# Three edits joined in a fused attention and routed feed-forward kernel: the last blocks' value products in a row, the last routing one half behind the other, four fill products at the branch's end

## The chip, the cores and the metric

The kernel runs on one core of a Trainium2 chip. The metric is the time of the device in microseconds (us), the median of several runs; lower is better. Five engines work in order, each on its own queue, and meet at semaphores: PE (TensorE, matrix products into PSUM), DVE (VectorE), ACT (ScalarE), POOL (GpSimd) and SP (SyncE, which issues most transfers). PE's clock has two levels, 2.4 GHz (a granted clock of 1.00 in the profile) and 1.2 GHz (0.50).

## What is computed

```python
# attention, for 4 batches x 8 heads, 768 tokens, head width 64
scores = q @ k.T / sqrt(64)
keep = (key position < n_sink) | (0 <= query - key < window)      # 4 and 128
a = softmax(where(keep, scores, -1e9)); x = a @ v                 # heads joined: 4 x 768 x 512
# routing, token by token
logits = x @ w_gate                                               # 8 experts
fresh = argmax(logits); local = sigmoid(x @ w_local)
e = fresh if first token or local < 0.5 else the expert of the token before
# one expert for each token
out = p[e] * (relu(x @ w1[e]) @ w2[e])                            # 512 -> 1024 -> 512, p = softmax(logits)
```

All in fp32. A product that needs fp32's precision is built from three products of halves: each operand is split into a high part (a cast, "fp32r") and a low part (the rest, a subtraction), and high x high, high x low and low x high are added up in PSUM.

## The kernel before

**Attention.** The 3072 tokens are 24 blocks of 128 per half of the heads, in 8 groups (4 batches x 2 halves of 4 heads), 48 blocks in all. Each block needs scores (L643), bias and mask on DVE (L655), exponentials on ACT (L658), transposes of them on PE (L673, copied by ACT at L680, `turned`), value products (L709, `apply`), a copy of those by DVE (L595, `collect`), a product that turns them back and gives the routing's logits (L599, `back`), and a division by the sums on DVE (L615, `ending`). The loop `for n in range(nb)` writes PE, DVE and ACT out by hand: in iteration n the scores of block n, the transposes of block n-1, the value products of block n-2 and the return of block n-3. POOL splits the next group's heads in the first two blocks of a group (L135, L140).

**Routing.** `routing()` returns small steps, most of them some DVE instructions on up to 48 elements: logits, `best`, `fresh`, `powers` (exponentials), a turn by PE and a `scan` for the expert carried on from token to token, `totals`, a turn back, `join` and `chosen` (the one-hot of the expert, L337 and L338), `gates` (L349 to L351), `ranks` (PE) and `slots`/`send`, and six scatters on POOL (L376), which write 128 rows each to a buffer in DRAM sorted by expert. The tables `ROUTE` and `ROUTE_L` say in which block behind a batch's last one each step is issued; the steps write into a free strip of a score bank. The last batch is routed in two halves, `head_r` and `tail_r`, in the straight code behind the loop.

**End of the attention branch.** That code handles the last three blocks (y, z, a), the two halves' routing, and work for expert 0 that can begin early: two blocks of its rows from the first three batches (`early_prep`: transposes L465, high part on ACT L468, low part on DVE L471) and six of the eight products with w1 (`early_first`, L489, 12 instructions each). At the end stand products with zeros (L1019), `FILL` of them, two instructions each, to keep PE at work. ACT's first cast behind the branch (L1302) waits until every engine has left it.

**Experts.** Behind the branch come the rest of expert 0's early blocks (L489 `hl`, then 48 products with w2, L1305), then a loop over 8 experts. Each is a `Switch` over arms by the number of 32-token groups; an arm issues the w1 products (L1185 or L1196), the w2 products (L1245) and, by an agenda of due times (`Agenda`, in estimated us), the splits of the weights of this and the next expert (`w_split`: high part on ACT L1101, low part on POOL or DVE L1102), the transposes of the next rows and the stores (`store`, L1221 to L1227). Between two arms `between()` loads the register that selects the next arm, sends a hint for its code, and issues 24 products with w2. Expert 0 has 308 tokens here, of which 256 are the early blocks; the arms taken are for 2 groups, then 8+7, 9, 11, 8+5, 5, 12+7 and 8+8.

## Time and profile before

| | before |
|---|---|
| median of 3 runs | 557.72 us (553.28 to 559.61) |
| profiled execution | 555.98 us, span 554.2 us, mean granted clock 0.975 |
| PE, DVE, ACT, POOL busy in the span | 94%, 60%, 50%, 42% |
| attention, to the end of the branch's fill | 0 to 221 us |
| arm of expert 0, and its 24 products | 238.0 to 252.9, to 260.2 us |
| arm of expert 3 (11 groups), and the products behind it | 337.4 to 372.6 us |
| experts 1 to 7 | 261.2 to 546.9 us |

A group of the page or a line of the timeline names the line of the kernel, the engine, the operation and its tiles; "idle before" is the time that the engine stood before it and what ended that. Busy PE does not mean PE at its peak, since products overlap and their ends are modelled. "issue" means that the profile shows nothing that was waited for.

### The profile page before, as it was taken

What the parts mean: (1) busy time and instruction counts of PE and PEld (TensorE: products, weight loads), DVE (VectorE), ACT (ScalarE), POOL (GpSimd) and SP (SyncE); (2) the same over time, 40 slices, a digit from 0 to 9 for tenths busy, and PEclk for the clock granted to TensorE, in tenths of its full rate; (3) what the DMA queues carried; (4) which work ended last, traced back from release to release, by engine and by line L of the source; (5) the groups of instructions that cost most, each with busy time, mean ns of one, the idle gap of its engine ahead of it and who ended that gap; (6) DMA issues with size and microseconds to landing.
All of it is one profiled execution on the core that took longest, in us unless ns stands there. A gap on an engine that the chain in (4) does not pass through costs nothing. (4 is left out here: it accounts for less than half of the span.)

```text
span 554.2 us, 11759 instructions
## 1 busy us (share of the span) xinstructions
PE 521.8 (94%) x3895; PEld 443.9 (80%) x3895; DVE 332.2 (60%) x1266; ACT 275.9 (50%) x839; POOL 233.0 (42%) x205
## 2 busy tenths in 40 slices
PE   8999999989999789989999999899999899999994
PEld 4788878878887576888987979779868598889893
DVE  6767898897888755623555383725455856443321
ACT  5878878867888721521632454506324453124110
POOL 5996373853843804340530342515304453104101
PEclk9999999998999989967999999999999999999998
DMA  8862404625260443753822556648325575120000
GB/s 283 286 224 68 184 29 175 189 93 179 71 255 21 150 138 128 240 163 105 289 83 63 190 174 218 214 135 287 97 45 187 191 239 209 39 58 25 20 25 36
DMA packets 31018, 80.46 MB, mean 145 GB/s; under 512 B 3678, under 2 KB 6366, under 8 KB 30816
## 3 DMA queue, kind: packets, MB, share of 16 engines
q1 hardware_dynamic: 26064, 65.41, 35.4%
q0 software_dynamic: 4176, 12.64, 6.0%
q14 instruction: 148, 1.21, 0.8%
q8 instruction: 54, 0.88, 0.7%
q10 hardware_dynamic: 576, 0.32, 0.2%
HBM read 63.34 MB, written 16.06 MB: 143 GB/s over the span
## 5 line engine op out<-in xcount | busy, mean ns | idle before, releaser
L658 ACT ACTIVATE pef<-smf,biasf 128x264 f32<-128x264 f32 (+2 forms) x192 | 93.7, 490 | 34.5 <-DVE biasf L655 33.3
L1207 ACT ACTIVATE hq<-h 128x32 fp32r<-128x32 f32 (+4 forms) x112 | 32.0, 316 | 150.4 <-PE h L1196 93.0
L1172 DVE SCALAR_TENSOR_TENSOR hq<-h,hq 128x32 fp32r<-128x32 f32 (+4 forms) x112 | 34.4, 332 | 69.6 <-ACT hq L1207 68.0
L1245 PE MATMUL late<-w_a,hq 128*128 128x512 f32 (+2 forms) x288 | 69.1, 394 | 1.7 <-issue 1.7
L655 DVE CUSTOM_DVE_ANT_0 smf<-sf,mask 128x264 f32<-128x264 f32 (+2 forms) x192 | 66.9, 402 | 4.5 <-PE sf L643 2.3
L1245 PEld LDWEIGHTS late<-w_a,hq 128*128 128x128 f32 (+2 forms) x288 | 50.7, 179 | 15.5 <-issue 2.6
L1227 POOL DMA_INDIRECT out_dram<-ot_d,oi_d x18 | 18.9, 1050 | 99.7 <-DVE ot_d L1226 79.8
L673 PE MATMUL tpf<-ident,pef 128*128 128x128 f32 x352 | 53.3, 284 | 2.4 <-ACT ptf L680 2.2
L680 ACT COPY ptf<-tpf 128x512 f32<-128x512 f32 (+1 forms) x96 | 51.0, 532 | 0.5 <-PE tpf L673 0.5
L709 PE MATMUL avf<-ptf,v 128*64 128x128 f32 x704 | 50.6, 286 | 0.0
L673 PEld LDWEIGHTS tpf<-ident,pef 128*128 128x128 f32 x352 | 37.5, 142 | 13.4 <-ACT ptf L680 7.2
L709 PEld LDWEIGHTS avf<-ptf,v 128*64 128x64 f32 x704 | 38.7, 140 | 4.7 <-issue 0.2
L376 POOL DMA_INDIRECT xs<-xb,slotf x24 | 23.8, 992 | 43.9 <-DVE row_i L408 20.9
L1245 PE MATMUL late<-w_b,hq 128*128 128x512 f32 (+1 forms) x168 | 41.2, 403 | 0.0
L1102 POOL TENSOR_TENSOR w_c<-raw,w_c 128x1024 fp32r<-128x1024 f32 x10 | 25.1, 2513 | 31.5 <-ACT w_c L1101 26.7
L1245 PEld LDWEIGHTS late<-w_b,hq 128*128 128x128 f32 (+1 forms) x168 | 31.9, 192 | 7.5
L1196 PEld LDWEIGHTS h<-x_a,w_c 128*128 128x128 f32 x288 | 34.8, 192 | 2.4 <-issue 2.3
L1196 PE MATMUL h<-x_a,w_c 128*128 128x256 f32 x288 | 35.2, 283 | 1.5 <-issue 1.1
L658 ACT ACTIVATION_READ_ACCUMULATOR pef<-smf,biasf 128x1 f32 x192 | 36.5, 190 | 0.0
L1102 POOL TENSOR_TENSOR w_a<-raw,w_a 128x1024 fp32r<-128x1024 f32 x10 | 24.7, 2473 | 27.2 <-ACT w_a L1101 24.9
L599 PE MATMUL bkf<-idw,xtf 128*128 128x146 f32 x192 | 32.6, 293 | 3.7 <-DVE xtf L595 3.6
L140 POOL TENSOR_TENSOR w_a<-raw,w_a 128x272 fp32r<-128x272 f32 (+4 forms) x22 | 29.4, 1352 | 5.6 <-ACT w_a L135 5.0
(236 smaller groups left out, 1066.3 us busy)
## 6 DMA issues: line engine op xcount, KB each, us to landing
raw<-in_dram SPq DMA_DIRECT2D x53, 512.0 KB, 5.2
raw<-in_dram SPq DMA_DIRECT2D x14, 800.0 KB, 5.9
xr_0n<-xs SPq DMA_DIRECT2D x21, 258.0 KB, 3.8
v<-in_dram SPq DMA_DIRECT2D x7, 768.0 KB, 4.4
raw_w<-in_dram SPq DMA_DIRECT2D x7, 512.0 KB, 5.1
raw<-in_dram SPq DMA_DIRECT2D x10, 256.0 KB, 4.8
xs<-zrow SPq DMA_DIRECT2D x9, 258.0 KB, 5.4
xr_0r<-xs SPq DMA_DIRECT2D x8, 258.0 KB, 3.3
```

What stands on the lines that cost most here:

```text
L140: return getattr(nc, e).tensor_tensor(out=out, in0=raw, in1=hi.bitcast(F32), op=ALU.subtract)
L599: mm = nc.tensor.matmul(bk[:, pr * WX:(pr + 1) * WX], blk["xt"][:, pr, :], idw[:, g * NPR + pr, :], start=True, stop=True, skip_group_chec ...
L655: u["dve"] = nc.vector.tensor_tensor_reduce(out=sm[:, :w], in0=sps[:, t, :w], in1=mk, scale=-0.125, scalar=BIG, op0=ALU.add, op1=ALU.min, ...
L658: nc.scalar.activation(pe[:, h, :w], sm[:, :w], AF.Exp, bias=bias[:, t:t + 1], scale=-1.0, accum_out=z[:, h, 0:1])
L673: nc.tensor.transpose(tp[:, t, k, :], pe[:, 2 * c + t, o:o + P], ident)
L680: nc.scalar.copy(pt[:, :, 0:nt, :], tp[:, :, 0:nt, :])
L709: nc.tensor.matmul(avt[ROWS[t], pr, :], prep["v"][:, j, 2 * pr + t, :], x["pt"][:, t, k, :], start=i < 2 and pr == 0 and k == 0, stop=pr = ...
L1102: todo += [lambda s=s: lo(out=l[:, s], in0=raw[:, s], in1=h.bitcast(F32)[:, s], op=ALU.subtract) for s in ([slice(0, FF)] if eng[1] == "po ...
L1172: nc.vector.scalar_tensor_tensor(out=d[:, :, 1, :], in0=h, scalar=0.0, in1=d.bitcast(F32)[:, :, 0, :], op0=ALU.max, op1=ALU.subtract)
L1196: nc.tensor.matmul(hs, w[:, k, fs], x, start=t == 0, stop=t == len(mm) - 1)
L1207: relu = nc.scalar.activation(d[:, :, 0, :], h, AF.Relu)
L1245: nc.tensor.matmul(o, a, w, start=t == 0, stop=t == len(mm) - 1, skip_group_check=half)
```

## The change

Six things change. (1) `ROUTE` and `ROUTE_L` are rewritten for a finer list of steps, in which `chosen` stands apart from the turn back: in the first two batches it is issued in the tenth block behind the batch (index 9) with `gates`, and in the third `gates` moves from index 8 to 7. The exponentials lie in nine columns, the ninth filled with 1e-9 once, so that one addition falls away. (2) The end of the branch is written anew: the last two blocks' value products follow each other, the turned logits of the first half come before them, the early rows and products behind; the first half's routing is finished before the second's begins; `hide` (the rest of `early_rows`) moves behind the copies; the fill has four products. (3) In `early_first` the order is high x high, low weight x high, high weight x low. (4) Only the first of three blocks of expert 0's rest rows is prepared ahead; the others come in the arm if it has them. Its second store moves into the arm. (5) `between` issues four products before the hint and the register load. (6) In wide arms, and for the next weights of long ones, the low parts go to POOL alone (`ALONE`) where POOL and DVE took turns.

On PE, at the end of the branch. Before, from the last block's return (`bkf` is the bank of returns, `avf` value products, `xpfe` the early rows, `hef` the early products, `encf` and `scf` the routing's turned values):

```order
L599 MATMUL bkf_3685<-idw,xtf_3673 128x146 x2
L465 MATMUL xpfe_3695<-ident,xr_178 128x128 x4
L704 MATMUL avf_0_3709<-ptsf_3635,srf_1_3193 128x128 x2
L709 MATMUL avf_0_3709<-ptf_1_4_0_3633,v_84 64x128 x4
L709 MATMUL avf_0_3709<-ptf_1_4_1_3643,v_84 64x128 x4
L465 MATMUL xpfe_3720<-ident,xr_179 128x128 x4
L489 MATMUL hef_3737<-x_a,w_a 128x256 x12
L704 MATMUL avf_1_3751<-ptsf_3691,srf_1_3193 128x128 x2
L709 MATMUL avf_1_3751<-ptf_1_5_0_3689,v_84 64x128 x4
L709 MATMUL avf_1_3751<-ptf_1_5_1_3693,v_84 64x128 x4
L599 MATMUL bkf_1_3762<-idw,xtf_0_3729 128x146 x2
L599 MATMUL bkf_2_3778<-idw,xtf_1_3765 128x146 x2
```

Now, from the same place:

```order
L604 MATMUL bkf_3679<-idw,xtf_3667 128x146 x2
L709 MATMUL avf_0_3683<-ptsf_3634,srf_1_3192 128x128 x2
L714 MATMUL avf_0_3683<-ptf_1_4_0_3632,v_84 64x128 x4
L714 MATMUL avf_0_3683<-ptf_1_4_1_3642,v_84 64x128 x4
L325 MATMUL bkf_h_3721<-ident,encf_3711 3x128
L709 MATMUL avf_1_3723<-ptsf_3703,srf_1_3192 128x128 x2
L714 MATMUL avf_1_3723<-ptf_1_5_0_3701,v_84 64x128 x4
L714 MATMUL avf_1_3723<-ptf_1_5_1_3705,v_84 64x128 x4
L604 MATMUL bkf_1_3736<-idw,xtf_0_3734 128x146 x2
L333 MATMUL bkf_h_3750<-ident,scf_0_3739 128x3
L334 MATMUL bkf_h_3750<-ident,scf_0_3739 128x3
L468 MATMUL xpf<-ident,xr_183 128x128 x4
```

The first early product and the early rows' transposes have left the value products; the first half's turn stands between them, and all the early products (`hef`) follow later, behind the first half's ranks.

On DVE, in the first block of a group in which the batch before is routed. Before:

```order
L333 SCALAR_TENSOR_TENSOR ends<-zrow,sf_1_0_1_1457 128x6
L334 TENSOR_TENSOR sif_0_1505<-sf_1_0_1_1457,ends 128x6
L337 TENSOR_SCALAR sif_0_1505<-sif_0_1505 128x6
L338 TENSOR_TENSOR ohs<-sif_0_1505,small 128x48
L615 TENSOR_TENSOR xb_154<-bkf_1486,rsf_0_3_0_1339 128x256
```

Now the two instructions on `sif` alone stand three blocks later, in front of `gates`:

```order
L611 TENSOR_REDUCE rsf_1_2_0_1709<-sum_z 128x4
L341 TENSOR_SCALAR sif_0_1508<-sif_0_1508 128x6
L342 TENSOR_TENSOR ohs<-sif_0_1508,small 128x48
L352 TENSOR_TENSOR ex_173<-ex_173,ohs 128x6x8
L353 TENSOR_REDUCE pgf_0_1713<-ex_173 128x6
```

Nothing else of that block changes its order; the copy for the value products (L595, now L600) follows the return of the block in both.

The core of the diff:

```diff
-FILL = 7
-ROUTE = 1, 3, 3, 4, 4, 5, 5, 6, 9, 10, 10, 11, 12, 13, 14, 15
-ROUTE_L = 1, 3, 3, 4, 4, 5, 5, 6, 8, 8, 8, 8, 9, 9, 10, 10
-EARLY = 9, 10, 11
+FILL = 4
+ROUTE = 1, 3, 3, 4, 4, 5, 5, 6, 9, 9, 10, 10, 11, 12, 13, 14, 15
+ROUTE_L = 1, 3, 3, 4, 4, 5, 5, 6, 6, 7, 8, 8, 8, 9, 9, 10, 10
+EARLY = 9, 10
...
+    ex_t = [rt.tile([P, NBLK, E + 1], F32, name=f"ex{x}") for x in range(2)]
+    for t in ex_t:
+        nc.gpsimd.memset(t, 1e-9)
...
+            t["ex"] = ex = ex_t[set2][:, 0:nb, 0:E]
...
-            nc.vector.tensor_reduce(out=sm, in_=t["ex"], axis=AX.X, op=ALU.add)
-            nc.vector.tensor_scalar(sm, sm, 1e-9, None, op0=ALU.add)
+            nc.vector.tensor_reduce(out=sm, in_=ex_t[set2][:, 0:nb], axis=AX.X, op=ALU.add)
...
-                part_of(turn, scan), part_of(read=totals), part_of(turn_back, one(join, chosen)), part_of(read=gates),
-                part_of(ranks, one(slots, send)), *out]
+                part_of(turn, scan), part_of(read=totals), part_of(turn_back, join), part_of(read=chosen),
+                part_of(read=gates), part_of(ranks, one(slots, send)), *out]
...
-        mm = [(w, a, k) for k in range(KC) for w, a in ((h1, 0), (h1, 1), (l1, 0))]
+        mm = [(w, a, k) for w, a in ((h1, 0), (l1, 0), (h1, 1)) for k in range(KC)]
...
+                head_r = routing(b, 0, LAST, sfx, True)
+                tail_r = routing(b, LAST, NBLK, sfx, True)
...
                 pack(a[0]["blk"], nm)
                 collect(y[0]["blk"], nm)
                 for u in a:
@@ -959,65 +973,62 @@
                 bk = ps_b.tile([P, 512], F32, tag="b", name=f"bk{nm}")
                 tps = sink_turn(a[0]["blk"], bk)
                 mm = back(g, y[0]["blk"], bk)
+                apply(z, f"{nm}_0")
+                reads(head_r, 0, 1)
                 turned(a[0])
                 lo = sink_out(a[0]["blk"], tps, mm, nm)
                 turned(a[1])
-                high0()
                 sums(a[0]["blk"])
+                reads(head_r, 2, 3)
                 ending(y[0]["blk"], NBLK - 3, bk)
                 lo()
                 invert(a[0]["blk"])
-                apply(z, f"{nm}_0")
-                high1()
-                low0()
+                head_r[4][0](bank("h4"))
+                apply(a, f"{nm}_1", ps_b.tile([P, 512], F32, tag="b", name=f"av{nm}_1")[:, 0:NPR * P].rearrange(
+                    "p (r c) -> p r c", r=NPR))
                 collect(z[0]["blk"], f"{nm}_0")
-                low1()
-                head_r[1][2]()
-                first_steps(0)
-                apply(a, f"{nm}_1")
                 bk = bank(1)
                 back(g, z[0]["blk"], bk)
+                reads(head_r, 4, 5)
+                first_rows[2][2]()
                 collect(a[0]["blk"], f"{nm}_1")
+                head_r[6][0](bank("h6"))
                 ending(z[0]["blk"], NBLK - 2, bk)
-                head_r[2][2]()
+                high0()
+                high1()
+                reads(head_r, 6, 7)
                 bk = bank(2)
                 back(g, a[0]["blk"], bk)
+                head_r[9][0](bank("h9"))
+                low0()
+                low1()
                 ending(a[0]["blk"], NBLK - 1, bk)
-                head_r[3][0](bank("h3"))
-                tail_r[0][2]()
-                head_r[3][1]()
-                first_steps(1)
-                tail_r[1][2]()
-                head_r[4][0](bank("h4"))
-                tail_r[2][2]()
+                first_steps(0, 1)
+                reads(head_r, 8, 9)
+                for st in head_r[10:]:
+                    st[2]()
+                reads(tail_r, 0, 1, 2, 3)
                 first_steps(2)
-                tail_r[3][0](bank("t3"))
-                head_r[4][1]()
-                tail_r[3][1]()
-                head_r[4][2]()
+                tail_r[4][0](bank("t4"))
+                reads(tail_r, 4, 5)
                 first_steps(3)
-                tail_r[4][0](bank("t4"))
-                head_r[6][0](bank("h6"))
-                tail_r[4][1]()
-                tail_r[4][2]()
-                head_r[5][2]()
-                head_r[6][1]()
-                for st in head_r[6:]:
+                tail_r[6][0](bank("t6"))
+                reads(tail_r, 6, 7)
+                first_steps(4)
+                tail_r[9][0](bank("t9"))
+                counts(ps_t, "t")
+                reads(tail_r, 8, 9)
+                for st in tail_r[10:]:
                     st[2]()
-                first_steps(4)
-                tail_r[6][0](bank("t6"))
-                counts(ps_t, "t")
-                tail_r[6][1]()
-                tail_r[5][2]()
-                for st in tail_r[6:]:
-                    st[2]()
-                low_steps(2)
+                metas0()
+                metas1()
                 masked()
+                low_steps(5)
                 first_steps(5)
                 fill = bank("fill")
                 for _ in range(FILL):
                     nc.tensor.matmul(fill, zrow[:, 0:P], zrow[:, 0:512], start=True, stop=True)
-                low_steps(4)
+                low_steps(1)
...
-        if hint is not None:
-            tc.switch_hint({x: hint for x in ORDERED}, len(GROUPS), f"arms{e + 1}")
-        v = ahead()
-        for _ in second(e, late_o[0], lambda f, a, n: hx[:, f, a * P:a * P + P], P):
-            pass
+        v = None
+        for t in second(e, late_o[0], lambda f, a, n: hx[:, f, a * P:a * P + P], P):
+            if t == 3:
+                if hint is not None:
+                    tc.switch_hint({x: hint for x in ORDERED}, len(GROUPS), f"arms{e + 1}")
+                v = ahead()
...
-    SHORT = (("act", "pool"),)
+    ALONE = (("act", "pool"),)
...
-    preps = [x_steps(t, xts[0], j, f"sn{j}", ps_x, "x") for j, t in enumerate(rows)]
+    first_prep = x_steps(rows[0], xts[0], 0, "sn0", room_x)
...
     products(range(0, 5))
-    preps[0][0]()
-    products(range(5, 6))
-    preps[1][0]()
-    products(range(6, FC))
-    preps[0][1]()
-    preps[1][1]()
-    preps[2][0]()
-    preps[2][1]()
+    first_prep[0]()
+    first_prep[1]()
+    products(range(5, FC))
+    first_prep[2]()
...
-    store_late(1, "_0")
...
-                    ag.add(2.5 * time1(ng) / FC, lambda: store_late(0, nm))
-                    t2 = 0.0
+                    for t in range(1 if e else NE):
+                        ag.add((2.5 + 2 * t) * time1(ng) / FC, lambda t=t: store_late(t, nm))
+                    t2, eng = 0.0, ALONE if time1(ng) > 12.0 else ENG
...
-                        step = min(2.0, time1(ng) / 4.5)
-                        w_agenda(ag, e, KC, NCH, 0.3, step, ENG)
+                        step = min(2.5 if eng is ALONE else 2.0, time1(ng) / 4.5)
+                        w_agenda(ag, e, KC, NCH, 0.3, step, eng)
...
-                                 ENG if e or span > 12.0 else SHORT)
+                                 ALONE if span > 24.0 or span <= 12.0 and not e else ENG)
```

## Rows read from the trace of the kernel before

**Rows 1.** The windows by stage, the window of experts 1 to 7. Columns: the stretch in us, its length, then for each engine the busy us (and the number of instructions), the granted TensorE clock, the DMA engines' busy share, GB/s.

```profile
261.00:547.00 286.00, 277.99 (x1624) 241.24 (x1624) 142.74 (x369) 105.11 (x267) 90.40 (x51) 1.00 0.41 136
```

**Rows 2.** The timeline (start us, us, engine, line, operation, output<-input, shapes, count, and in brackets the idle time before it and what ended it) of POOL, DVE and PE in the attention loop, and among them the view of line 349 (`gates`) with count, and min/median/max in ns. L338 is the second step of `chosen`; L140 is the low part of a head's split.

```profile
75.41 3.66 POOL L140 TENSOR_TENSOR w_a<-raw,w_a 128x768 fp32r<-128x768 f32 x2
...
75.54 1.76 DVE L338 TENSOR_TENSOR ohs<-sif,small 128x48 bf16<-128x48 int32 x1
...
122.17 1.83 DVE L338 TENSOR_TENSOR ohs<-sif,small 128x48 bf16<-128x48 int32 x1
...
168.45 0.21 DVE L338 TENSOR_TENSOR ohs<-sif,small 128x48 bf16<-128x48 int32 x1
...
L349 DVE TENSOR_TENSOR exf<-exf,ohs x3: 196/198/1248, 86.5 to 175.5; 128x48 f32<-128x48 f32 x3
...
78.77 0.77 PE L599 MATMUL bkf<-idw,xtf 128*128 128x146 f32 x4 [1.10 <-DVE xtf L595]
...
125.48 0.77 PE L599 MATMUL bkf<-idw,xtf 128*128 128x146 f32 x4 [2.53 <-DVE xtf L595]
177.46 0.63 PE L643 MATMUL sf<-hq 64*128 64x264 f32 x6 [1.12 <-DVE slf L363]
```

**Rows 3.** The timeline of PE: the scores that begin four blocks of attention, and the window by stage behind the second of the gaps above (columns as in rows 1).

```profile
121.38 0.98 PE L643 MATMUL sf<-hq 64*128 64x256 f32 x12
131.93 0.39 PE L643 MATMUL sf<-hq 64*128 64x264 f32 x2
...
146.93 0.97 PE L643 MATMUL sf<-w_a 64*128 64x256 f32 x12
153.15 0.64 PE L643 MATMUL sf<-w_a 64*128 64x264 f32 x5
...
128.00:130.00 2.00, 2.00 (x16) 1.69 (x15) 1.17 (x6) 0.72 (x4) 2.00 (x2) 0.50 0.32 71
```

**Rows 4.** Who PE waited for from 189 to 222 us: what waited and for whom, us in total, times, longest us.

```profile
PE bkf L684 <- DVE pkf L663: 2.3, 1, 2.3
PE tpf L673 <- ACT ptf L680: 1.0, 1, 1.0
PE hef L489 <- ACT x_a L468: 0.7, 1, 0.7
PE bkf_t L360 <- DVE cum L372: 0.5, 1, 0.5
PE bkf_h L321 <- DVE exf L316: 0.5, 1, 0.5
PE hef L489 <- ACT hq L493: 0.4, 1, 0.4
PE hef L489 <- DVE x_a L471: 0.3, 1, 0.3
```

**Rows 5.** The timeline of DVE, PE, POOL and ACT at the end of the attention branch. L449 is `hide`, L709 the value products, L1019 the fill, L368 the slots of the tail, L376 the scatters, L1302 the first cast behind the branch.

```profile
190.19 2.42 DVE L449 TENSOR_SCALAR hide<-early_g 128x2 int32<-128x2 f32 x1
...
187.94 1.09 PE L709 MATMUL avf<-ptf,v 128*64 128x128 f32 x16
195.95 1.98 PE L709 MATMUL avf<-ptf,v 128*64 128x128 f32 x16
214.73 6.17 PE L1019 MATMUL bkf_fill<-zrow 128*128 128x512 f32 x14
...
215.67 0.17 DVE L368 TENSOR_REDUCE slotf<-slf 128x3 int32<-128x24 f32 x1
...
213.47 0.99 POOL L376 DMA_INDIRECT xs<-xb,slotf  x1 [20.89 <-DVE row_i L408]
219.83 0.96 POOL L376 DMA_INDIRECT xs<-xb,slotf  x1 [0.31 <-issue]
...
220.66 1.14 ACT L1302 CAST w_b<-raw 128x512 fp32r<-128x512 f32 x2 [5.34 <-DVEq L1321]
```

**Rows 6.** The timeline of PE behind the branch: one block of rows transposed between two runs of products (start to start).

```profile
228.52 0.60 PE L465 MATMUL xpsn<-ident,xrsn 128*128 128x128 f32 x4
228.87 1.18 PE L1305 MATMUL late<-w_b,hq 128*128 128x512 f32 x4
```

**Rows 7.** A group of the page (the low parts of weight chunks on POOL: busy us, mean ns of one, idle before and what ended it), and the timeline of DVE and PE in the arm of the fourth expert. L1102 is the low part of a weight chunk, L465 the transposes of a block of rows.

```profile
L1102 POOL TENSOR_TENSOR w_a<-raw,w_a 128x1024 fp32r<-128x1024 f32 x10 | 24.7, 2473 | 27.2 <-ACT w_a L1101 24.9
...
345.97 2.61 DVE L1102 TENSOR_TENSOR w_b<-raw,w_b 128x512 fp32r<-128x512 f32 x1
...
349.78 0.63 PE L465 MATMUL xp_0n<-ident,xr_0n 128*128 128x128 f32 x4 [1.70 <-issue]
```

**Rows 8.** Who PE waited for from 221 to 548 us (columns as in rows 4); L1245 are products with w2, L1196 with w1.

```profile
PE late L1245 <- issue: 2.8, 3, 1.2
PE h L1196 <- issue: 2.1, 2, 1.1
```

**Rows 9.** The arm of expert 0 and the 24 products behind it: the timeline of PE, a window by stage, and the same kind of 24 products behind the next expert.

```profile
237.97 9.34 PE L1185 MATMUL h<-x_b,w_a 128*128 128x128 f32 x48 [1.53 <-issue]
...
240.00:250.00 10.00, 10.00 (x49) 10.00 (x49) 3.13 (x15) 3.53 (x10) 5.68 (x3) 0.50 0.52 168
...
252.87 7.30 PE L1245 MATMUL late<-w_b,hq 128*128 128x512 f32 x24
303.05 5.72 PE L1245 MATMUL late<-w_a,hq 128*128 128x512 f32 x24 [1.23 <-issue]
```

More of the change, by code (lines that the diff above doesn't have):

```diff
@@ L952, in low_steps, with reads @@
                         lows_f.pop(0)()
-                head_r[0][2]()
+                def reads(r, *ks):
+                    for k in ks:
+                        r[k][1]()
                 pack(a[0]["blk"], nm)
@@ L1402, in flush @@
                     ag.run(0.0, True)
+            for j in range(1, (groups[0] + 3) // 4) if not e else ():
+                for f in x_steps(rows[j], lead, j, f"{nm}s{j}", room_x):
+                    f()
             xt, blk = lead, 0
```

42 lines of the change are left out of this document (25 added, 17 removed).

## The prediction

> **What bounds the kernel now.** I read the windows by stage first. From 261 to 547 us, in experts 1 to 7, PE is busy 277.99 of 286 us at a granted clock of 1.00, which is 2.4 GHz [rows 1]: PE bounds the kernel there, and at most 8 us of gaps can be won. In general time can only come from PE's gaps, from PE work that goes, or from stretches at the lower of its two levels, 1.2 GHz (0.50). So I read PE's timeline for its gaps next, and for each gap what DVE and POOL did just before. Three places stand out: stalls of DVE in the attention loop [rows 2, 3], the end of the attention branch [rows 4, 5], and the boundaries of the experts, further down.
>
> **Attention: routing steps that meet a POOL pass.** A DVE instruction on a few dozen elements takes 1.76 and 1.83 us in the first two batches, where POOL runs subtractions of heads at the time (75.41 to 79.07 for the first), and 0.21 us, the same line, at 168.45; `gates` shows it too, 0.20 us twice and 1.25 us once [rows 2]. PE then stands 1.10, 2.53 and 1.12 us: twice for the value copy that DVE owes it, once for the score bank that the routing step still reads. The change takes `chosen` out of the first block of a group, where POOL splits heads, to the fourth, where `gates` already stands; and in the third batch `gates` one block earlier. The order on DVE above shows the first of these. DVE's work there does not grow, and `gates` ran there unhindered in both batches (0.20 us). So the gaps of 1.10 and 1.12 us go. The 2.53 us gap cost more than itself: right behind it the granted clock is 0.50 [rows 3], and the two blocks of scores from 121.38 to 131.93 took 10.55 us where the same two of the next group, 146.93 to 153.15, took 6.22: 4.33 us. Term: 1.10 + 4.33 + 1.12 = **6.55 us**. Below it is zero, if the moved steps meet a POOL pass again; above 7.2, if DVE's backlog behind a gap costs a little more. I take 6.55, since each part is a gap read on PE itself. The reduction over nine columns instead of eight plus one addition drops one DVE instruction per routing, the three new memsets stand in POOL's idle start: nothing.
>
> **The end of the branch.** PE's waits from 189 to 222 us sum to 5.7 us [rows 4]: 2.3 for `pkf`, which stood on DVE behind the `hide` instruction of 2.42 us [rows 5], 1.0 for the copies on ACT, 1.0 for the early rows' copies in `x_a`, and 1.4 for steps of the routing and a PSUM bank. The change sends `hide` behind the copies, both value products one behind the other, the early rows behind the turned logits, and the routing of the first half before all of the first expert's early products. The 1.0 on ACT stays. The other 4.7 go, but two waits come in: the last value product waits for the low part of the sinks (some 0.4 us on DVE by my count of its order), and the fill waits until DVE has read the tail's ranks, because they share a bank (some 0.5 us). Net 3.8. The half-clock stretch from 195 to 198 goes with the gap before it: sixteen value products took 1.98 us there and 1.09 before [rows 5], with the transposes 1.4 us. Three of seven fills go: 14 instructions took 6.17 us, so 0.88 each, 2.6 us. Term: 3.8 + 1.4 + 2.6 = **7.8 us**. Below: the gap at `pkf` and the fills alone, 4.9. Above: all waits, the clock and the fills, 9.7.
> What is late next there is POOL. Its six scatters follow each other every 1.27 us from 213.47 to 219.83, the first three waiting for a routing that could be done long before, and ACT's first cast of the second weights starts behind the last, at 220.66 [rows 5]. With the first half's routing in front, its scatters leave some 12 us earlier, and the last three hang on the tail's slots alone. Those were ready at 215.84 [rows 5]. PE's rank products come earlier by the term without the fills and their wait, 5.7 us, and about 0.5 us of DVE work in front of the slots (the sums, done earlier) goes: 209.6. Some 0.4 us later POOL starts, its last scatter 2.5 us behind, and the cast 0.83 behind that as before: 213.4. PE leaves its last fill at 213.1, and has 3 us of products of its own before it needs a cast. So the cover holds; it is gone when the slots come more than 2 us later than this. ACT, DVE and the row loads on SP stand behind the same scatters and move with them.
>
> **Two blocks of rows not prepared.** Only the first rest block of expert 0 is transposed ahead. Between the products a block costs PE 0.35 us [rows 6], two of them **0.7 us**; ACT and DVE shed casts and subtractions that nobody waits for. Expert 0 has one rest block here (its arm starts with 64 columns), so none comes back in the arm. `store_late(1)` moves into the arm, where DVE has room.
>
> **Subtractions from DVE to POOL.** For wide arms the low parts of the weights go to POOL alone. In the fourth expert PE stood 1.7 us at a row transpose, because DVE's release of the bank stood behind one such subtraction of 2.61 us (it also met a POOL pass) [rows 7]; without it DVE is there in time: **1.7 us**. Below it could cost: a POOL pass is 2.47 us, eight of them 19.8 us [rows 7]; the arm lasts 36 us with the products behind it (the table above), so POOL stays inside, and I count no loss, with 2.5 us (one late pass) as the other end.
> The Trainium skill, "GPSIMD Engine Reference", section "4.1 Engine selection", says of adds on a tile to take VectorE and not GpSimd, about twice as slow for two inputs. By that rule alone this part would be a loss; the trace agrees on the single pass, but here the cover decides, and the sum with the rule would lack the 1.7 us.
>
> **Hint and register load behind four products.** At the end of an arm PE stood three times, 2.8 us in all, before the first of the 24 products [rows 8]; now four products (some 0.95 us, a sixth of the 5.72 us that 24 take [rows 9]) can run in front of the load. But the hint for the next arm leaves as much later, and entries stand 2.1 us in two and 1.53 us in one case already [rows 8, 9]. From 2.4 us gained to 6.7 lost (0.95 at seven entries): I take **zero**, since the gaps show no cause but "issue".
> The Trainium skill, "Runtime: NRT & Kernel Launch", section "Instruction fetch mechanics", gives about 0.2 us for a register load, which would make the gain here an estimated 0.6 us; no row shows the load itself.
>
> **Sum.** 6.55 + 7.8 + 0.7 + 1.7 = 16.75 us. Against the profiled execution of 555.98 us that is 539.2. It lay 1.7 us below the median of the runs shown, 557.72, and the runs spread over 6.3; against the median: **541 us**.
>
> **Rivals.**
> *The clock stays up in expert 0's arm.* Its products are narrow; PE stood 1.53 us before them, and the granted clock was 0.50 behind that [rows 9]. The change shifts this place and not its kind, so I leave it. Should the clock stay at 1.00, the 24 products behind the arm take 5.72 instead of 7.30 us, and its 64 narrow ones, 0.195 us each (48 took 9.34) and 12.5 in all, save between nothing and half; with 5 us of that, 6.6 us: **534**.
> *The routing of the tail hardly gains.* If the tail's slots come 5 us later than I count, POOL ends late and ACT's cast and PE's products behind it move with it: 4.9 instead of 7.8, **544**. For it: the chain is long, with DVE and PE by turns.
> *The moved steps meet POOL again, so the change does not do what it says:* zero instead of 6.55, **547.5**. Against it: `gates` in the same block [rows 2].
> *POOL becomes the late one in wide arms:* 1.7 gained become 2.5 lost, and once more in the seventh expert: **547**.
> *Slower: the hint too late.* Each entry stands 0.95 us longer, and where the sum then is as long as the 1.53 us before expert 0's arm, the clock falls as there. It lasted some 17 us there: from the arm's products, which begin at 237.97, to about 256, since the 24 products behind took 1.58 us more than their like, which is 3.2 us at half [rows 9]. That costs a wide arm up to 8.5 us. One such entry makes 541 + 6.7 + 8.5 = 556, no difference; from two on it is slower, **565**. For it: two entries of about 1.05 us stand there now [rows 8]. Against: 1.7 us of standing in the fourth expert left the clock at 1.00 [rows 1, 7].
>
> **Chances.** Forecast 0.50; clock up 0.15; tail 0.13; moved steps 0.07; POOL late 0.05; the hint with no or one fall 0.06; with two or more 0.04. The first five are faster by more than 1% (about what a measurement of this kernel can tell), save what the spread of runs takes: faster 0.88, same 0.08, slower 0.04. The forecast's own range, with the ends of its terms, is 537 to 546; to leave out no more than 2 in 10 the range reaches to the clock rival below and to the moved steps above: 531 to 549.
>
> **What would show it.** Right: no DVE instruction of `chosen` or `gates` above 0.3 us in the loop and no PE gap above 0.5 us there; clock 1.00 from 120 to 235 us of the old places; the first scatter of the last batch ten microseconds or more before the last; ACT's first cast some 14 us earlier than 220.66; no gap of 1.7 us in the fourth expert. Wrong: a PE gap of several microseconds between fills and the next product; POOL passes that end after the products need them; entries into arms that stand 2 us and a clock of 0.50 behind a wide one.

## The result and the profile after

The changed kernel takes **534.57 us** (median of 4 runs, 532.70 to 538.01) where the kernel before takes 556.11 (4 runs): the ratio is 0.9617, 95% interval 0.9538 to 0.9696. (A ratio in this document is that of the mean times, without runs more than 1.5% above the fastest of their kernel.) The profiled execution took 534.75 us, its span 532.9 us, at a mean granted clock of 0.991 (before 0.975). The time lies in the range of the prediction, 6.4 us below the forecast of 541.

PE stays the bound in experts 1 to 7. The window of [rows 1] in the profile after:

```profile
243.00:526.00 283.00, 277.58 (x1624) 240.80 (x1623) 126.83 (x341) 105.01 (x267) 122.18 (x66) 1.00 0.42 141
```

It does the same 1624 instructions; 16 us of DVE's work has gone to POOL, where it takes 32. Where the other time went is read from PE's timeline, from the same product in both (columns as in rows 2):

```profile
182.15 1.09 PE L714 MATMUL avf<-ptf,v 128*64 128x128 f32 x16
...
186.31 1.09 PE L714 MATMUL avf<-ptf,v 128*64 128x128 f32 x16
...
188.96 1.09 PE L714 MATMUL avf<-ptf,v 128*64 128x128 f32 x16
...
196.15 3.14 PE L494 MATMUL hef<-x_a,w_a 128*128 128x256 f32 x24 [0.53 <-ACT hq L498]
...
205.11 3.59 PE L1030 MATMUL bkf_fill<-zrow 128*128 128x512 f32 x8
208.81 3.11 PE L494 MATMUL hl<-x_a,w_a 128*128 128x256 f32 x24
211.82 4.84 PE L1324 MATMUL late<-w_b,hq 128*128 128x512 f32 x20
...
223.33 5.52 PE L1203 MATMUL h<-x_b,w_a 128*128 128x128 f32 x48
230.28 1.11 PE L468 MATMUL xp_0n<-ident,xr_0n 128*128 128x128 f32 x4 [1.43 <-DMA xr_0n<-xs]
231.04 3.65 PE L1203 MATMUL h<-x_b,w_a 128*128 128x128 f32 x16
...
236.08 5.88 PE L1263 MATMUL late<-w_b,hq 128*128 128x512 f32 x24
242.75 11.75 PE L1214 MATMUL h<-x_a,w_c 128*128 128x256 f32 x96 [0.79 <-PE late L1263]
```

| up to | before | after | won in this part | forecast |
|---|---|---|---|---|
| the loop's last value products | 187.94 | 182.15 | 5.79 | 6.55 |
| `hl`, behind the fill | 221.00 | 208.81 | 6.40 | 7.8 |
| the end of the early blocks' products | 236.44 | 223.49 | 0.76 | 0.7 |
| expert 1's first product | 261.22 | 242.75 | 5.52 | 0 (rival: 6.6) |
| first product of expert 4, the one behind the fourth expert | 373.65 | 353.33 | 1.85 | 1.7 |
| the last product's end | 546.87 | 525.59 | 0.96 | 0 (with the gaps of `between`) |

The six parts sum to 21.3 us, the difference of the spans. (236.44 is where these products end in the kernel before; its entry into the arm, 1.53 us later in [rows 9], counts to the arm. Experts are numbered from 0, so the fourth expert is expert 3.)

The stalls of DVE are gone from the loop. `chosen` (now L342) and `gates` (L352), with count and min/median/max in ns:

```profile
L342 DVE TENSOR_TENSOR ohs<-sif,small x3: 207/209/209, 85.2 to 163.7; 128x48 bf16<-128x48 int32 x3
L352 DVE TENSOR_TENSOR ex<-ex,ohs x3: 200/210/211, 85.4 to 166.7; 128x48 f32<-128x48 f32 x3
```

What PE waited for from 183 to 209 us (columns as in [rows 4]), and from 242 to 540 us:

```profile
PE tpf L678 <- ACT ptf L685: 1.0, 1, 1.0
PE xpf L468 <- ACT x_a L469: 0.7, 1, 0.7
PE avf L709 <- DVE ptsf L699: 0.6, 1, 0.6
PE hef L494 <- ACT hq L498: 0.5, 1, 0.5
PE hef L494 <- issue: 0.4, 1, 0.4
PE bkf_h L325 <- DVE ex L320: 0.4, 1, 0.4
...
PE h L1214 <- PE late L1263: 1.5, 2, 0.8
PE h L1214 <- issue: 1.4, 1, 1.4
PE h L1203 <- PE late L1263: 0.8, 1, 0.8
...
PE late L1263 <- issue: 0.7, 2, 0.5
```

The 2.3 us behind `hide` of [rows 4] have gone, the 1.0 us on ACT has stayed, and a new wait of 0.7 stands before the second block of early rows. And POOL's first scatter of the last batch now leaves 11.7 us ahead of the last, with ACT's first cast behind them:

```profile
196.83 0.99 POOL L379 DMA_INDIRECT xs<-xb,slotf  x1 [9.94 <-DVE lgf L299]
...
208.52 0.96 POOL L379 DMA_INDIRECT xs<-xb,slotf  x1 [0.30 <-issue]
211.15 1.14 ACT L1321 CAST w_b<-raw 128x512 fp32r<-128x512 f32 x2 [5.45 <-PEq L1340]
```

### The profile page after: what moved, and what is told of

Read it like the earlier page. It is cut to its first block, busy times and chain, and to the rows that moved or that the text cites. A ratio compares the mean times of both kernels' runs of the same rounds, so it can differ in the third digit from the quotient of the medians.

```text
span 532.9 us, 11724 instructions
## 1 busy us (share of the span) xinstructions
PE 508.8 (95%) x3881; PEld 434.0 (81%) x3881; DVE 306.1 (57%) x1227; ACT 274.5 (52%) x837; POOL 265.1 (50%) x222
## 5 line engine op out<-in xcount | busy, mean ns | idle before, releaser
L1245 POOL DMA_INDIRECT out_dram<-ot_d,oi_d x18 | 18.4, 1021 | 85.2 <-DVE ot_d L1244 65.8
L714 PE MATMUL avf<-ptf,v 128*64 128x128 f32 x704 | 49.0, 279 | 0.0
L1116 POOL TENSOR_TENSOR w_c<-raw,w_c 128x1024 fp32r<-128x1024 f32 x14 | 33.4, 2402 | 24.1 <-PE h L1203 8.4
L1116 POOL TENSOR_TENSOR w_a<-raw,w_a 128x1024 fp32r<-128x1024 f32 x12 | 29.8, 2496 | 24.0 <-ACT w_a L1115 18.3
L1116 POOL TENSOR_TENSOR w_b<-raw,w_b 128x1024 fp32r<-128x1024 f32 x14 | 33.6, 2407 | 15.9 <-ACT w_b L1115 10.3
L714 PEld LDWEIGHTS avf<-ptf,v 128*64 128x64 f32 x704 | 37.4, 136 | 4.7 <-issue 0.2
L1263 PE MATMUL late<-w_b,hq 128*128 128x512 f32 (+1 forms) x168 | 39.8, 393 | 0.0
```

Source lines behind the costliest of these rows:

```text
L714: nc.tensor.matmul(avt[ROWS[t], pr, :], prep["v"][:, j, 2 * pr + t, :], x["pt"][:, t, k, :], start=i < 2 and pr == 0 and k == 0, stop=pr = ...
L1116: todo += [lambda s=s: lo(out=l[:, s], in0=raw[:, s], in1=h.bitcast(F32)[:, s], op=ALU.subtract) for s in ([slice(0, FF)] if eng[1] == "po ...
L1263: nc.tensor.matmul(o, a, w, start=t == 0, stop=t == len(mm) - 1, skip_group_check=half)
```

## The experiments

Medians compare on one chip; the runs of one kernel spread over 3 to 11 us, so what an edit did is read from its place in the profile first.

### The loop alone

```diff
 (the kernel before)
-ROUTE = 1, 3, 3, 4, 4, 5, 5, 6, 9, 10, 10, ...
-ROUTE_L = 1, 3, 3, 4, 4, 5, 5, 6, 8, 8, 8, 8, 9, 9, 10, 10
+ROUTE = 1, 3, 3, 4, 4, 5, 5, 6, 9, 9, 10, 10, ...
+ROUTE_L = 1, 3, 3, 4, 4, 5, 5, 6, 6, 7, 8, 8, 8, 9, 9, 10, 10
```

(and `chosen` as a step of its own.)

> The kernel before with the new tables for the routing steps alone (and the step of the one-hot apart); the end of the branch and all behind it as before. Theory: the three stalls of DVE at 75, 122 and 175 us and with them PE's gaps of 1.10, 2.53 and 1.12 us go, and the half clock behind the second; PE reaches its first product behind the loop 5.8 us earlier, the rest is unchanged (entry of expert 0's arm 1.5 us, half clock in it): 5.8 us less than the kernel before. Rival: the steps meet another pass of POOL in their new blocks, or what PE wins it waits for ACT at the loop's end: less than 2 us won.

Measured: 549.07 us against 553.66, ratio 0.9949 (0.9855 to 1.0042). By the runs alone it could be no change; the place in the profile decides. PE's rows show the loop's last value products at 181.57 instead of 187.94, 6.4 us sooner, no gap of 1 us in the loop behind its first group, and the two others of the last blocks as far apart as before to within 0.2 us, the first of them at half clock:

```profile
181.57 1.09 PE L709 MATMUL avf<-ptf,v 128*64 128x128 f32 x16
...
189.73 1.98 PE L709 MATMUL avf<-ptf,v 128*64 128x128 f32 x16
...
195.62 1.09 PE L709 MATMUL avf<-ptf,v 128*64 128x128 f32 x16
```

Expert 0's arm was entered behind a stand of 2.07 us, at half clock, as the theory had it.

### The routing steps put back

```diff
 (the changed kernel)
-ROUTE = 1, 3, 3, 4, 4, 5, 5, 6, 9, 9, ...
-ROUTE_L = 1, 3, 3, 4, 4, 5, 5, 6, 6, 7, ...
+ROUTE = 1, 3, 3, 4, 4, 5, 5, 6, 6, 9, ...
+ROUTE_L = 1, 3, 3, 4, 4, 5, 5, 6, 6, 8, ...
+                first_rows[2][2]()
                 pack(a[0]["blk"], nm)
...
-                first_rows[2][2]()
                 collect(a[0]["blk"], f"{nm}_1")
```

> The changed kernel with three places of the routing put back to where they met POOL's passes: the one-hot in the first block of a group again (first two batches), the gates of the third batch one block later, and the step that takes the rest of the early rows (one DVE instruction on 128x2 numbers) at the head of the branch's end again, where POOL subtracts from 184.4 to 186.9 us. Theory: DVE instructions of a few dozen elements take 1.2 to 2.4 us there again, PE stands about 1.1, 2.5 and 1.1 us in the loop and 2 us at its end, with half clock behind two of these: 5.8 us in the loop and 2.3 to 3.7 at its end, 8 to 9.5 us more than the changed kernel. Rival: the end was bound by the chain of the routing, not by this step; then 5 to 6 us more.

Measured: 549.36 us, against 556.60 for the kernel before on this chip (ratio 0.9919, 0.9866 to 0.9972): of the change's 21 us some 7 are left by the medians, some 4.5 by the ratio. DVE's and PE's rows:

```profile
76.34 1.84 DVE L342 TENSOR_TENSOR ohs<-sif,small 128x48 bf16<-128x48 int32 x1
79.65 1.34 PE L604 MATMUL bkf<-idw,xtf 128*128 128x146 f32 x4 [2.40 <-DVE xtf L600]
...
125.76 1.83 DVE L342 TENSOR_TENSOR ohs<-sif,small 128x48 bf16<-128x48 int32 x1
129.06 0.77 PE L604 MATMUL bkf<-idw,xtf 128*128 128x146 f32 x4 [2.69 <-DVE xtf L600]
...
179.05 1.27 DVE L352 TENSOR_TENSOR ex<-ex,ohs 128x48 f32<-128x48 f32 x1
181.02 0.64 PE L648 MATMUL sf<-hq 64*128 64x264 f32 x6 [1.15 <-DVE slf L366]
...
193.75 2.40 DVE L452 TENSOR_SCALAR hide<-early_g 128x2 int32<-128x2 f32 x1
196.75 0.29 PE L689 MATMUL bkf<-ident,pkf 128*96 128x128 f32 x1 [1.81 <-DVE pkf L668]
```

The stalls come back at each of the four places, and only there. The cost is above the theory's 8 to 9.5: the loop's last value products begin at 191.50, 9.35 us later than in the changed kernel, and the last of all at 199.95, 11.0 later. The loop's share is larger than the 5.8 expected, and the end's, 1.65, smaller than 2.3 to 3.7: the clock stayed at 1.00 there. This time the first gap was nearly as long as the second, and the clock was at 0.50 behind both. That what they meet is POOL's pass is in the same profile: POOL subtracts on 128x768 elements from 74.46 to 78.13 and from 123.88 to 127.53, and on 128x512 from 177.74 to 180.25 and from 193.62 to 196.12. The Trainium skill, "SBUF — State Buffer", section "SBUF: two separate sides", names a reason, a pair of ports that a DVE instruction in a 2-port mode or with two inputs in SBUF and a GpSimd instruction hold against each other for its whole length. The rows agree for L342 and L352, which have two inputs; `hide` (L452) has one and stalls 2.40 us all the same, and no row shows whether it runs in such a mode.

### Fills

```diff
-FILL = 4
+FILL = 0
```

> No fill products at the end of the branch, the rest is the changed kernel. Theory: the four fills (8 instructions, 3.59 us) cover the time until ACT's first cast of the second weights, which came at 211.15 us, 0.67 us before PE's first product with it, and which hangs on POOL's last scatter (209.5) and on new code, not on PE. Without them PE stands some 3 us before that product, wins nothing, and may drop to half clock behind the stand: 536 to 540. Rival: the cast waits for PE to leave the branch; then it comes earlier with PE, by up to 1.7 us, and 1 to 3 us are won: 534.

Measured: 533.11 us (before on this chip 553.66). PE and the cast in the timeline:

```profile
195.31 3.13 PE L494 MATMUL hef<-x_a,w_a 128*128 128x256 f32 x24 [0.53 <-ACT hq L498]
...
207.13 4.54 PE L494 MATMUL hl<-x_a,w_a 128*128 128x256 f32 x24 [2.72 <-DVE hq L499]
...
209.77 1.14 ACT L1321 CAST w_b<-raw 128x512 fp32r<-128x512 f32 x2 [4.94 <-PEq L1340]
...
211.47 4.81 PE L1324 MATMUL late<-w_b,hq 128*128 128x512 f32 x20
```

The window by stage behind the stand (columns as in rows 1):

```profile
208.00:211.00 3.00, 3.00 (x17) 3.00 (x16) 0.00 (x0) 1.23 (x3) 0.63 (x1) 0.54 0.54 194
```

At its place the theory holds in size, not in cause: this execution was 0.84 us ahead at the early products (195.31 against 196.15) and 0.35 ahead at the first late product, so dropping 3.59 us of fills lost 0.5 us. PE stood 2.72 us, before `hl` and not before the late product as I wrote, and the clock fell to half. It was DVE's `hq` that PE stood for, not the cast, which began 1.70 us ahead of the first late product. In the profile the time is low for another reason: in expert 0's arm nothing stood this time (below).

With `FILL = 7`:

> Seven fill products at the end of the branch, as in the kernel before; the rest is the changed kernel. Theory: six instructions more of 0.44 us, 2.6 us, and nothing behind them comes sooner: 2.6 us more than the changed kernel. Rival: ACT's first cast is what PE then meets in any case, and ACT comes later in most executions than in the one profiled: under 1 us more.

Measured: 536.58 us. The first late product begins at 215.09, where the early products had begun 0.78 us later than in the changed kernel (196.93): 2.5 us more, against 2.6 expected. ACT's cast came at 211.41, before PE's last fill had ended. So three more fills are lost time. With four, the first late product begins 0.67 us behind the start of its cast (211.82 and 211.15 above).

### Blocks of rows prepared ahead

```diff
-    first_prep[0]()
-    first_prep[1]()
-    products(range(5, FC))
+    preps[0][0](); preps[0][1]()
+    products(range(5, 6))
+    preps[1][0](); preps[1][1]()
+    products(range(6, FC))
...
+    store_late(1, "_0")
```

> All three blocks of expert 0's rest rows are transposed ahead again and the second store stands ahead of the arm again, as in the kernel before; the rest is the changed kernel. Theory: two blocks of 0.35 us on PE, 0.7 us, and PE enters expert 0's arm without standing, as in the changed kernel: 0.7 us more. Rival: the 1.53 us at the entry of this arm in the kernel before came with these blocks and the store (their waits on ACT and DVE, their code); then it stands 1 to 1.5 us again, the clock is at 0.50 from there on for some 15 us, and the time is 5 to 8 us more.

Measured: 537.57 us. The first two blocks cost 0.35 and 0.36 us from start to start, as forecast, but the third stood 2.25 us for DVE (223.44 us), which the kernel before did not show, so this is not that kernel's price; the clock was at 0.50 behind it for some 3 us. PE entered the arm at 229.20 without a stand: the rival falls, blocks and store did not make the entry late. What did stays open.

### The hint in front again

```diff
-        for t in second(...):
-            if t == 3:
-                tc.switch_hint(...)
-                v = ahead()
+        tc.switch_hint(...)
+        v = ahead()
+        for _ in second(...):
+            pass
```

> The hint and the register load go in front of the 24 products again, as in the kernel before; the rest is the changed kernel. Theory from the two profiles: the four products cover the register load; in front of the products PE then stands about 2.8 us in all again instead of 0.7, and at the entries as long as in the changed kernel (3.8 in all): 534.6 + 2.1 = 536.7. Rival, the forecast's: what the load costs in front the earlier hint gives back at the entries, which then stand 2 us less in all: 534.6.

Measured: 536.72 us, and 536.98 for the changed kernel beside it: no difference. Its waits from 240 to 540 us:

```profile
PE late L1263 <- issue: 3.5, 3, 1.5
PE h L1214 <- PE late L1263: 1.3, 2, 0.7
...
PE h L1203 <- PE late L1263: 0.5, 1, 0.5
```

In front of the products PE stands 3.5 us instead of 0.7, and at the entries 1.8 instead of 3.7 (1.5, 1.4 and 0.8 above). The rival, which was the forecast, is nearer: most of what the load costs comes back. Whether the 0.9 us left over are real these two profiles cannot tell. From expert 1 on the two kinds of stand sum to 5.0 to 6.6 us in the three profiles with the hint in front (before, loop alone, this one) and to 3.0 to 6.6 in the eleven others. The estimate of 0.6 us, worked out in the prediction from the Trainium skill's "Runtime: NRT & Kernel Launch", section "Instruction fetch mechanics", cannot be told from zero either.

### Low parts on both engines again

```diff
-                    t2, eng = 0.0, ALONE if time1(ng) > 12.0 else ENG
+                    t2, eng = 0.0, ENG
...
-                                 ALONE if span > 24.0 or span <= 12.0 and not e else ENG)
+                                 ENG if e or span > 12.0 else ALONE)
```

> The low parts of the weights alternate between POOL and DVE in all arms again. Theory: in the fourth expert the row transpose waits again for DVE behind a subtraction of 2 us or more, 1.7 us; with it the two entries around it, 534.6 + 2.2 = 536.8. Rival 1: that gap hung on when POOL and DVE met and not on the list, no gap comes back: 534.6. Rival 2: POOL alone costs elsewhere (the wait of 0.73 us for DVE in the second expert, 1.44 us at the seventh's entry) as much as it wins: 534.6 or less, with the gap at the fourth expert back.

Measured: 540.49 us against 536.98 beside it (ratios to the kernel before 0.9777, 0.9711 to 0.9844, and 0.9718, 0.9643 to 0.9794). In the fourth expert:

```profile
328.30 2.62 DVE L1116 TENSOR_TENSOR w_b<-raw,w_b 128x512 fp32r<-128x512 f32 x1
...
332.11 0.63 PE L468 MATMUL xp_0n<-ident,xr_0n 128*128 128x128 f32 x4 [1.67 <-issue]
```

The gap is back with its subtraction; from this expert's first product to its first with w2 it takes 18.68 us instead of 16.79. Of the 3.5 us of the medians this place shows 1.9; the rest is inside the spread. In return a wait is gone that POOL alone had brought, in the second expert of the changed kernel:

```profile
276.86 0.66 PE L468 MATMUL xp_0n<-ident,xr_0n 128*128 128x128 f32 x4 [0.73 <-DVE x_b L476]
```

It stands in all eleven profiles with POOL alone, at 0.72 to 0.75 us, and in none of the three with both engines (before, loop alone, this one). In each of the eleven, two DVE instructions on 128x96 elements took 2.65 us some 7 us ahead of it (269.46 in the changed kernel), beside a POOL pass of 2.51. So the second rival is right in part: POOL alone has a price elsewhere.

### Expert 0's arm

The changed kernel was run twice more, with no edit.

> The changed kernel once more, with a second profile, beside the variants below on the same chip. My theory of expert 0's arm: its narrow products fall to half clock only behind a stand of PE of more than a microsecond; so the profile shows 1.00 until PE stands about 1.4 us for the next expert's rows, 0.50 for some 6 us behind that, and about 534.6 us. Rival: where the clock falls in this arm changes from execution to execution, and the 5.5 us that the arm gained were partly luck: then the fall lies elsewhere in this profile, lasts up to 17 us, and the time is up to 539.

Measured: 536.98 us (the third time, on another chip, 537.26). In both profiles the clock fell at or behind the stand for the rows, as the theory had it, but it stayed down for some 10 and 13 us instead of 6, and PE stood 3.19 and 2.32 us more in front of the 24 products. From PE's entry into this arm to expert 1 it took 22.7 and 24.1 us where the first profile has 19.4 (table below). So the rival is right too: what the arm gained was partly luck.

Next the write of zeros goes out earlier:

```diff
     pad(0)
+    pad(1)
...
-    pad(1)
     products(range(0, 5))
```

> The write of zeros behind expert 1's rows goes out right behind the one for expert 0, ahead of three loads of 512 KB, instead of behind them. Theory: the loads of expert 1's rows wait until this write has landed (27 us of SP's queue show it idle for 7 us between the two); early, the rows are there when PE wants them, the stand of 1.43 us goes, the clock stays at 1.00 in the arm and 22 products there (16 with rows, 8 transposes and some more) take half of their 6 us: 534.6 - 1.4 - 3.1, about 530. Rival 1: the narrow products alone bring the clock down; it falls in the arm though nothing stands, and only 1.4 us is won: 533. Rival 2: the row loads wait for SP's own entry into the arm or for a free buffer: the stand stays, 534.6.

Measured: 536.16 us. The write left at 208.42 us instead of 220.43, and SP still sent the loads of expert 1's rows only at 228.77, 5.2 us behind the last load ahead of them; PE stood 0.56 and 0.59 us. So it was not that write that they waited for; rival 2 stands, and SP's own entry into the arm is what is left. The clock stayed at 1.00, so the narrow products alone did not bring it down, and rival 1 falls. How long PE stands follows from when SP sends these loads, counted from PE's first product in the arm. Where they left 3.38 to 4.78 us behind it, the stand was 2.74 to 2.82 us less than that, in six profiles of seven (3.17 us at 4.45 with the steps put back). Where they left at most 2.43 us behind it (fill 0, fill 7, blocks ahead), nothing stood.

So the loads themselves were put ahead of the arm, with the zeros as above:

```diff
+    rows1 = lead_rows(1)
+    tiles1 = [x_rows(r, f"an{j}") for j, r in enumerate(rows1)]
     products(range(0, 5))
```

In the run called best, `high1()` moves behind `back(g, a[0]["blk"], bk)` too.

> The changed kernel with two steps moved. (a) The write of zeros for expert 1 and the loads of expert 1's first rows leave SP's queue ahead of expert 0's arm instead of inside it. (b) At the branch's end the second block of early rows is transposed behind the last block's return instead of in front of it. Theory for (a): the stand of 1.1 to 1.9 us for these rows in expert 0's arm brought the clock to 0.50 there; with the rows in time nothing stands, the clock stays at 1.00 and the time from PE's entry into this arm to its entry into the next is 15 to 16 us (18.8 to 22.7 where PE stood): 3.5 us less than the changed kernel, at least. Rival: the rows come in time, and the clock falls all the same, since the products are narrow: about 1.4 us less. For (b): the stand of 0.68 us before that block (PE waits for ACT's copy of the first) goes and PE's early products start 0.5 us sooner against the loop's end; or, since these need the second block's copy too, they start as late as before, and the wait moves to them.

Measured: 534.61 us (before on this chip 556.60). For (a) nothing stood in the arm, but PE stood 3.52 us in front of the 24 products, and behind that the clock was at 0.50 for some 3 us: 19.3 us from entry to entry, not 15 to 16. For (b) the wait only moved: the early products begin 4.59 us behind the last value products, as in the changed kernel. Then part (a) alone, beside the changed kernel.

> The changed kernel a third time, on the same chip as the next one, to compare the two by their runs: 534 to 537 us.

> The changed kernel with the zeros for expert 1 and the loads of expert 1's rows ahead of expert 0's arm (part (a) of the run called best, alone). Theory: nothing stands in the arm, the clock stays at 1.00 there, and the runs are 2 to 3.5 us shorter than the changed kernel's of the same chip. Rival: PE then comes to the end of the arm before the code behind it is there and stands 3 us or more in front of the 24 products (3.52 in the profile of the run called best), and the runs are the same within 1 us.

Measured: **533.64 us** (531.50 to 539.87), the changed kernel 537.26 (532.95 to 539.75) on the same chip, the kernel before 554.61. The ratios to the latter are 0.9592 (0.9530 to 0.9654) and 0.9658 (0.9595 to 0.9720): 3.6 us between the medians, with intervals that overlap. The arm in the timelines of the two profiles, first the changed kernel:

```profile
230.57 1.12 PE L468 MATMUL xp_0n<-ident,xr_0n 128*128 128x128 f32 x4 [1.99 <-DMA xr_0n<-xs]
231.34 3.65 PE L1203 MATMUL h<-x_b,w_a 128*128 128x128 f32 x16
...
239.04 7.51 PE L1263 MATMUL late<-w_b,hq 128*128 128x512 f32 x24 [2.32 <-issue]
```

The window over the arm's second half in it:

```profile
230.00:236.00 6.00, 5.43 (x26) 5.43 (x27) 2.08 (x12) 1.13 (x4) 3.07 (x3) 0.50 0.84 289
```

Then with the rows ahead:

```profile
230.72 1.99 PE L1203 MATMUL h<-x_b,w_a 128*128 128x128 f32 x16
...
236.02 5.76 PE L1263 MATMUL late<-w_b,hq 128*128 128x512 f32 x24 [2.42 <-issue]
```

And its window:

```profile
230.00:236.00 6.00, 3.60 (x33) 3.34 (x32) 4.37 (x21) 2.27 (x7) 4.53 (x4) 1.00 0.64 211
```

Theory and rival are both half right: the clock stays, sixteen products take 1.99 us instead of 3.65, and PE stands 2.42 us behind the arm, for nothing that the profile shows. Sending the zeros early has a price too: in this profile and in that of the zeros early, PE's first late product stood 0.69 and 0.35 us for ACT, whose cast had last waited for that write. The profiles of all kernels give one table:

| profile | stood at or in the arm, us | clock behind it | stood before the 24 products | entry to expert 1, us |
|---|---|---|---|---|
| before; loop alone | 1.53; 2.07 | 0.50 | none | 24.8; 25.5 |
| after; its two repeats | 1.43; 1.85; 1.99 | 0.50 | none; 3.19; 2.32 | 19.4; 22.7; 24.1 |
| steps put back; hint in front; both engines | 3.17; 1.31; 1.09 | 0.50 | none; 1.73; none | 21.1; 22.8; 18.8 |
| zeros early | 0.56 and 0.59 | 1.00 | none | 16.8 |
| fill 0; fill 7; blocks ahead | none | 1.00 | none; none; 0.20 | 15.4; 15.8; 15.8 |
| best; rows ahead | none | 1.00 | 3.52; 2.42 | 19.3; 17.7 |

(The last column counts from the arm's first product, and the stand ahead of it, where there is one, is added.) In eight profiles PE stood 1.09 us or more there, and the clock was at 0.50 behind it, at once or up to 2 us later; in six it did not, and the clock stayed. Moving the loads is the only intervention among them, and it went the same way, in two profiles.

## Why the prediction was right, and where not

**Attention, 6.55: right.** 5.79 us measured in the change, 6.4 in the loop alone; put back, the stalls return at their places. The half clock behind the second gap is a matter of the execution: put back, it stood behind two gaps.

**End of the branch, 7.8: mechanism right, mis-sized.** 6.40 measured. The three fills gave 2.58 (6.17 less 3.59, forecast 2.6), and the half clock went (1.4). The term that was mis-sized is "net 3.8" for the waits: it is 6.40 - 2.58 - 1.4 = 2.4. Of the two waits that I said would come in, the sinks' is there with 0.57 and the fill's is not; but the 0.68 before the second block of early rows came in as well, and the 0.53 and 0.42 among the early products and 0.37 at the first half's turn stayed, where I had let all of their kind go. One stall of the very kind that the change removes came in, and the prediction overlooked it. With `hide` gone from the head of the branch's end, a step of the first half's routing meets POOL's last subtraction (184.37 to 186.88 us); the same line takes 0.18 us in the second half:

```profile
185.87 1.06 DVE L306 TENSOR_TENSOR eqf<-lgf,mxf 128x24 f32<-128x24 f32 x1
...
196.88 0.18 DVE L306 TENSOR_TENSOR eqf<-lgf,mxf 128x24 f32<-128x24 f32 x1
```

It takes 0.96 to 1.15 us in eleven profiles of the new end, and 0.18 only where `hide` stood in front again. What PE waited 0.37 and 0.57 us for stands behind it on DVE; that these two waits come from it is argued from that order, no run took it away.

**POOL's chain** came out of the same step: the tail's slots were ready 1.9 us later than I counted (205.72 us, 211.5 with the loop's 5.79 added back, for 209.6), and ACT's cast not 0.83 but 2.6 us behind the last scatter, so that it came 9.5 and not 14 us earlier. What the cast waited for in these 2.6 us is not known; in the twelve profiles of the new end it begins 2.0 to 3.4 us behind the last scatter. My 3 us of cover at PE was used up: the cast began 0.67 us ahead of PE's first late product, and with the zeros early and the rows ahead, where it came later, PE stood 0.35 and 0.69 us for ACT.

**Two blocks, 0.7: right** (0.77). **Subtractions to POOL, 1.7: right at its place**, the gap gone and back when undone. But I counted no loss, and the 0.73 us in the second expert came with it, so the term is nearer to 1.0; the rest of the 1.85 up to expert 4 are shorter stands in front of products and entries. The rule of the Trainium skill, "GPSIMD Engine Reference", section "4.1 Engine selection", by which this was a loss, holds for the single pass (DVE 0.68 us on half a chunk where POOL does not interfere, POOL 2.4 on a whole one) and did not decide. **Hint, zero: right as far as it can be told.** The measured gain from expert 4 on is 0.96, and it lies inside what these stands vary by between the profiles.

**Expert 0's arm, zero: wrong**, and its 5.52 us is more than the 4.5 by which the sum, 16.75, fell short of the 21.3 between the two profiles; loop and branch's end gave 2.2 less than forecast and hid part of it. The step that failed is "the change shifts this place and not its kind, so I leave it". The entry's 1.53 us did not come again in any of the twelve profiles with the new end, and the clock held until PE stood for the next expert's rows. The rival had 6.6 us, and the mechanism (clock up, 24 products in 5.88 instead of 7.30); it assumed no stand inside the arm, and its price without one is larger than I wrote: 24.8 us, the entry's 1.53 among them, become 15.4 to 15.8. But the 5.52 us are partly luck: in the two repeats this arm gained 2.1 and 0.7 us, and their medians, 536.98 and 537.26, lie nearer to the forecast.

**The rival of falling clocks** had the condition that a stand as long as 1.53 us brings the clock down at a wide arm too. The entry to the seventh expert stood 1.44 us in the profile after and up to 1.95 in its repeat, with a clock of 1.00 behind: that condition does not hold there. Longer stands did bring it down in front of products of 512 columns, 2.25 us with the blocks ahead and 3.52 in the run called best, each for some 3 us, and 2.42 with the rows ahead did not. The stretch that this rival took for its price is also longer than written: 237.97 to 256 are 18 us and not 17, so up to 9 us for a fall and not 8.5; that changes no bound.

## What to carry to other kernels

A DVE instruction on a few dozen elements that takes 2 us in one block and 0.2 in another is not slow, it is blocked: look at what POOL does in the same microseconds, and move the step to a block where POOL is idle. Then look for what the move brings to POOL's next pass: here another step of the routing stalled there, and the subtractions that POOL took over stalled DVE in the second expert. Price a gap on PE with the clock behind it, read from rows of the same place: behind 1.09 us and more in expert 0's arm it was at 0.50 and cost several us, behind 1.42 to 1.95 at the seventh expert's entry it stayed at 1.00. And when a wait in front of a stage goes, read in the same timeline which load the stage itself will wait for next; here it was the next expert's rows, issued inside the arm. A gain that depends on such a wait needs more than one profile.

## What the runs showed of the hardware

The same stand is followed by half clock in one execution and not in another. At 28.7 us, where PE waits 1.45 us for POOL's first split in every profile, the clock was at 0.50 behind it in six of the thirteen profiles of the variants and of the changed kernel, and at 1.00 in the others. The Trainium skill, "TensorE: Matmul & The Clock Gate", section "Part 1: The HAM clock gate", says that one kernel's count of slow products varies between runs; these profiles agree. Part of the spread of 3 to 11 us between runs of one kernel is therefore likely to be the clock; only one execution per kernel has a trace, so that is argued and not shown.

Code that PE comes to behind a short arm can be late: the 24 products behind expert 0's arm stood 1.73 to 3.52 us in five of the fourteen profiles, with no releaser shown, and at most 0.20 in the nine others. The cause was not found.
